# Batch 0 of a fused sigmoid attention and ReGLU kernel: values four passes behind scores, value casts on GpSimd, keys in two pieces, zero matmuls in gaps, and the last columns in two banks

## The chip, the cores and the metric

The kernel runs on one core of one Trainium2 chip. The metric is the device time of one execution in microseconds (us), as the median over repeated executions. Besides it there is the **span** that a profile shows, from the first to the last instruction of the execution that was profiled.

## The reference, cut to what matters

```python
def _attn_ref(q, k, v):                       # q, k, v: (8, 12, 448, 64) float32
    scores = np.matmul(q, k.transpose(0, 1, 3, 2)) / np.sqrt(64) - np.log(448)
    attn = 1.0 / (1.0 + np.exp(-scores))      # sigmoid, no softmax
    return np.matmul(attn, v)

def _moe_ref(x, w_gate, w_val, w_out):        # x: (3584, 768), d_ff = 1536
    gate = np.maximum(x @ w_gate, 0.0)
    return (gate * (x @ w_val)) @ w_out       # (3584, 768) float32
```

The output of the attention, heads side by side, is the input x of the second part, called the FFN below. Its product with `w_out` is the **down projection**.

## The kernel before: the parts concerned

Twelve heads of a batch are three blocks of four heads, so there are 24 blocks. A block is worked off in seven **passes**, one for each group of 64 keys: scores on TensorE (PE), the sigmoid on ScalarE (ACT), values on TensorE. Batch 0 (blocks 0 to 2, 21 passes) is a stage of its own. From then on the FFN of batch b runs on TensorE, and the passes of batch b + 1 are slipped in as **visits** between its matmuls.

```python
filler(40)                                   # 40 matmuls of 128 columns on the identity
cast_qk(0, "q", nc.vector, nc.scalar)
cast_qk(0, "k", nc.vector, nc.scalar)
for _ in range(4):
    start_next()                             # next weight load, and its cast on GpSimd
transposes(0, "q", nc.vector)
transposes(0, "k", nc.scalar, nc.vector)
cast_v(0, nc.vector)

LAG = 2
for i in range(NBLK * NCH + LAG):            # batch 0
    n, c = divmod(i, NCH)
    if n < NBLK:
        scores(n, c)
    if i >= LAG:
        m, cm = divmod(i - LAG, NCH)
        values(m, [cm])
    ...                                      # casts and transposes of block n + 1
    if i % 2 == 1 and i < NBLK * NCH:
        start_next()

def visit():
    i0 = state["pass"]
    n, c = divmod(i0, NCH)
    i1 = min(i0 + (3 if c == 0 else 2), NPASS)
    for i in range(i0, i1):
        if c == 0 and i == i0 + 2 and n > NBLK:
            values(n - 1, range(NCH))
        scores(*divmod(i, NCH))
    ...
```

`feed`, called by each visit, loads and casts later blocks. Blocks 3 to 5 are transposed on TensorE, blocks from 6 on by DMA. Loads are issued in program order, those of the first three blocks on two queues, all later ones on one. The last columns of the output are copied out of one bank of PSUM (the memory that TensorE writes its results to), half by ACT, half by VectorE (DVE).

## Time and profile before

| | the kernel before |
|---|---|
| median of the timed executions | 434.59 us (434.58 to 435.0) |
| the profiled execution: time | 437.15 us |
| the profiled execution: span | 434.6 us |
| TensorE busy | 421.6 us (97%) |
| first sigmoid starts, last sigmoid starts | 8.23, 26.66 us |
| first FFN matmul | 28.25 us |

The page itself has a sign of what was particular about that execution, the granted TensorE clock in tenths, over 40 slices of the span:

```profile
PEclk9989999999999999999999999999999999999999
```

The 8 in the third slice (21.7 to 32.6 us) means that the clock was not full there for part of the time.

The timeline of the last microseconds of the same profile shows the tail: start, length, engine, instruction, and in brackets the idle time before it with what ended it.

```profile
430.89 0.28 ACT L268 ACTIVATE ysb<-y_ps 128x128 f32<-128x128 f32 x1 [0.66 <-PE y_ps L251]
431.20 0.29 DVE L269 TENSOR_SCALAR ysb<-y_ps 128x128 f32<-128x128 f32 x1 [15.22 <-ACT ysb L268]
```

DVE waited for ACT, not for TensorE: both read the same PSUM bank, one after the other.

### The profile page before, as it was taken

The page shows a single profiled execution, that of the slowest core. Times are in us where ns is not written, and L with a number is a line of the kernel's source. Part 1 is how long each engine was busy: PE and PEld are TensorE (multiplying, and loading weights), DVE is VectorE, ACT ScalarE, POOL GpSimd, SP SyncE. Part 2 cuts the span into 40 slices and gives each one's busy share as a digit, 9 for nine tenths or more (in the row PEclk, how much of TensorE's full clock was granted, in tenths as well). Part 3 has the DMA queues.
Part 4 walks back from the last instruction along what each step waited for, and adds up shares of the span by engine and source line. Part 5 has one row for each costly group of instructions (what it writes and reads, how often), then busy time and mean ns, then how long its engine had stood idle before and what let it go on. Part 6 is the DMA issues. An engine that isn't in the chain of part 4 may idle for free.

```text
span 434.6 us, 7877 instructions
## 1 busy us (share of the span) xinstructions
PE 421.6 (97%) x3292; PEld 216.9 (50%) x3292; DVE 102.8 (24%) x172; ACT 235.6 (54%) x325; POOL 100.6 (23%) x130
## 2 busy tenths in 40 slices
PE   7779999999999999999999999999999999999996
PEld 5334554544455445544455454554455444455553
DVE  3632331123201322113211232023220232212210
ACT  5955656655566555555546556565555556532221
POOL 0287758213301313113031133023130100000000
PEclk9989999999999999999999999999999999999999
DMA  8999999791228910596216932199114320030014
GB/s 306 385 384 386 391 391 271 221 265 72 42 74 231 301 37 16 144 262 170 42 38 193 255 128 44 42 242 293 21 24 109 80 44 2 14 96 1 2 36 110
DMA packets 64100, 66.98 MB, mean 154 GB/s; under 512 B 35776, under 2 KB 54336, under 8 KB 64064
## 3 DMA queue, kind: packets, MB, share of 16 engines
q1 hardware_dynamic: 63088, 64.89, 51.2%
q10 hardware_dynamic: 976, 1.57, 1.0%
q8 instruction: 26, 0.43, 0.4%
q14 instruction: 10, 0.08, 0.1%
HBM read 47.19 MB, written 11.01 MB: 134 GB/s over the span
## 4 chain that ended last, share of the span: by engine, by line
PE 95%; ACT 4%; issue 1%; POOL 0%; DVE 0%; ACTq 0%; POOLq 0%
PE gv_ps L225 51%; PE y_ps L251 26%; PE qk_ps L172 9%; PE pv_ps L196 7%; ACT PT L182 3%; PE tr L157 1%; PE fill L336 1%; ACT gate_sb L237 0%; ACT kT L162 0%; POOL ident masks.py:199 0%; DVE ysb L269 0%; ACT ysb L268 0%; POOL ident masks.py:197 0%; POOL bias_t L63 0%; ACTq L182 0%
## 5 line engine op out<-in xcount | busy, mean ns | idle before, releaser
L182 ACT ACTIVATE PT<-qk_ps,bias_t 128x896 f16<-128x896 f32 x168 | 158.1, 1006 | 55.9 <-PE qk_ps L172 55.7
L225 PE MATMUL gv_ps<-xT,wg 128*128 128x448 f16 x576 | 128.5, 355 | 0.0
L225 PE MATMUL gv_ps<-xT,wv 128*128 128x448 f16 x576 | 128.3, 354 | 0.0
L251 PE MATMUL y_ps<-wo,hT 128*128 128x512 f16 (+1 forms) x672 | 114.1, 326 | 0.0
L237 ACT ACTIVATE gate_sb<-gv_ps 128x448 f32<-128x448 f32 x96 | 52.3, 544 | 93.5 <-PE gv_ps L225 93.5
L240 DVE TENSOR_TENSOR hT<-gate_sb,gv_ps 128x448 f16<-128x448 f32 x96 | 59.6, 621 | 168.7 <-PE gv_ps L225 135.8
L251 PEld LDWEIGHTS <-hT 128*128 128x128 f16 x672 | 64.0, 98 | 48.1 <-issue 7.5
L225 PEld LDWEIGHTS <-wv 128*128 128x128 f16 x576 | 54.8, 98 | 57.1 <-issue 9.1
L225 PEld LDWEIGHTS <-wg 128*128 128x128 f16 x576 | 55.0, 98 | 54.6 <-issue 7.1
L209 DVE TENSOR_SCALAR xT<-pv_ps 128x448 f16<-128x448 f32 x48 | 27.7, 620 | 133.1 <-PE pv_ps L196 133.0
L172 PE MATMUL qk_ps<-qT,kT 64*64 64x448 f16 x672 | 51.6, 360 | 6.6 <-ACT PT L182 6.0
L116 POOL CAST v<-st_v 128x448 f16<-128x448 f32 x21 | 11.8, 562 | 173.2 <-PE pv_ps L196 172.6
L273 ACT ACTIVATE ysb<-y_ps 128x512 f32<-128x512 f32 (+1 forms) x55 | 27.1, 493 | 40.6 <-PE y_ps L251 40.3
L196 PE MATMUL pv_ps<-PT,v 64*64 64x448 f16 x672 | 40.2, 351 | 1.3 <-ACT PT L182 0.8
L172 PEld LDWEIGHTS <-kT 64*64 64x64 f16 x672 | 15.8, 105 | 37.3 <-issue 33.0
L109 POOL CAST h16q<-st_q 128x896 f16<-128x896 f32 x21 | 19.6, 932 | 33.3 <-DMA kT<-h16k 32.5
L196 PEld LDWEIGHTS <-v 64*64 64x64 f16 x672 | 20.1, 107 | 13.5 <-issue 1.8
L109 POOL CAST h16k<-st_k 128x896 f16<-128x896 f32 x21 | 19.6, 932 | 1.3 <-DMA qT<-h16q 0.8
L141 POOL CAST wg<-st_wg 128x1536 f16<-128x1536 f32 x6 | 8.9, 1484 | 18.1 <-DMA st_wg<-in_moe_w_gate_dram 18.1
L117 POOL CAST v<-st_v 64x448 f16<-64x448 f32 x21 | 11.7, 559 | 1.3
L118 POOL CAST v<-st_v 64x448 f16<-64x448 f32 x21 | 11.7, 557 | 0.9
L141 POOL CAST wo<-st_wo 128x1536 f16<-128x1536 f32 x6 | 8.8, 1468 | 6.2 <-DMA st_wo<-in_moe_w_out_dram 6.2
(28 smaller groups left out, 51.6 us busy)
## 6 DMA issues: line engine op xcount, KB each, us to landing
st_q<-in_q_dram SPq DMA_DIRECT2D x24, 448.0 KB, 4.7
out_dram<-ysb SPq DMA_DIRECT2D x54, 192.0 KB, 2.7
st_v<-in_v_dram SPq DMA_DIRECT2D x23, 448.0 KB, 5.9
st_k<-in_k_dram SPq DMA_DIRECT2D x22, 448.0 KB, 5.2
st_wg<-in_moe_w_gate_dram SPq DMA_DIRECT2D x6, 768.0 KB, 11.9
st_wu<-in_moe_w_val_dram SPq DMA_DIRECT2D x6, 768.0 KB, 12.2
st_wo<-in_moe_w_out_dram SPq DMA_DIRECT2D x6, 768.0 KB, 11.9
st_k<-in_k_dram ACTq DMA_DIRECT2D x2, 448.0 KB, 6.6
```

Of the source, the lines that this page charges most:

```text
L109: eng.tensor_copy(o, i)
L116: eng.tensor_copy(t[:, 0], st[:, 0])
L141: eng.tensor_copy(dst, st[:])
L172: nc.tensor.matmul(ps[o : o + 64, bank, 0:S], kT[r : r + 64, c, h, :], qT[r : r + 64, :, h, :], start=True, stop=True, tile_position=(r, o ...
L182: nc.scalar.activation(pt[:], ps[:, :, 0:S], AF.Sigmoid, bias=bias_t[:], scale=qk_scale)
L196: nc.tensor.matmul(pv[pr][o : o + 64, 0:S], t[r : r + 64, pr, c * D : (c + 1) * D], pt[r : r + 64, pr, :], start=(c == 0), stop=(c == NCH ...
L209: nc.vector.tensor_scalar(out=x[:], in0=pv[pr][:, 0:S], scalar1=XSCALE, scalar2=None, op0=AOP.mult)
L225: nc.tensor.matmul(acc[:, 0:S], w[:, dc, jj * P : (jj + 1) * P], xT[b, dc][:], start=(dc == 0), stop=(dc == NDC - 1),)
L237: nc.scalar.activation(g_sb[:], acc[:, 0:S], AF.Relu)
L240: nc.vector.tensor_tensor(out=hT[f][:, o : o + S], in0=g_sb[:], in1=ps[1][:, 0:S], op=AOP.mult)
L251: nc.tensor.matmul(y[:, 0:mn], hT[f][:, o : o + P], wo[f // FG][:, f % FG, m0 : m0 + mn], start=(f == 0), stop=(f == NFC - 1),)
L273: nc.scalar.activation(ysb[:, m0 : m0 + mn], y[:, 0:mn], AF.Copy, scale=OUT_SCALE)
```

## The change

Its intent is to make the start of the FFN earlier and the end shorter. In batch 0 the values run four passes behind the scores (two at the end), the casts of the values move from DVE to GpSimd (POOL), block 0's keys are loaded and cast in two pieces, and zero matmuls fill gaps on TensorE to keep its clock up. The first FFN visit has two passes instead of three, block 6 is transposed on TensorE instead of by DMA, and the last 256 columns go to two banks. Cut to its core:

```diff
     def feed(i: int):
...
-        if c == 4 and NPRO <= m < NB:
+        if c == 4 and NPRO < m < NB:
             dma_transposes(m)
-        if c == 5 and NBLK < m < NPRO:
+        if c == 5 and NBLK < m <= NPRO:
             transposes(m, "k")
             transposes(m, "q")
...
-        i1 = min(i0 + (3 if c == 0 else 2), NPASS)
+        i1 = min(i0 + (3 if c == 0 and n > NBLK else 2), i0 + NCH - c, NPASS)
...
-        filler(40)
-        cast_qk(0, "q", nc.vector, nc.scalar)
-        cast_qk(0, "k", nc.vector, nc.scalar)
+        new_fill()
+        filler(*[512] * 10)
+        cast_qk(0, "q", nc.vector, nc.scalar, cut=(0, 4, NCH))
+        cast_qk(0, "k", nc.vector, nc.scalar, cut=(0, 2, 4))
+        transposes(0, "q")
+        filler(128, 128)
+        transposes(0, "k", nc.scalar, nc.vector, cut=(0, 2, 4))
...
+        cast_qk(0, "k2", nc.vector, cut=(4, NCH))
+        for n in range(NBLK):
+            cast_v(n, nc.gpsimd)
...
-        LAG = 2
-        for i in range(NBLK * NCH + LAG):
+        NP0 = NBLK * NCH
+        done = 0
+        for i in range(NP0 + 2):
             n, c = divmod(i, NCH)
             if n < NBLK:
                 scores(n, c)
-            if i >= LAG:
-                m, cm = divmod(i - LAG, NCH)
-                values(m, [cm])
+            while done <= i - (4 if i < NP0 - 4 else 2):
+                values(done // NCH, [done % NCH])
+                done += 1
...
+            if 1 <= i <= 3:
+                filler(256)
...
-            if c == 4 and n + 1 < NBLK:
-                transposes(n + 1, "k")
-                transposes(n + 1, "q")
-                cast_v(n + 1, nc.vector)
-            if i % 2 == 1 and i < NBLK * NCH:
+            if c in (3, 5) and n + 1 < NBLK:
+                transposes(n + 1, "k" if c == 3 else "q")
+            if 13 <= i < NP0:
                 start_next()
...
-                count = 3 * NBLK + (1 if b == 0 else 0)
+                count = 3 * NBLK + (2 if b == 0 else 0)
```

Cut out: the loads of k in two pieces, the two banks in `down`, and the order k before q in later loads.

More of the change, by code (lines that the diff above doesn't have):

```diff
@@ L86, in load_block, with cast_qk @@
         b, i = divmod(n, NBLK)
-        for nm, src, eng in which:
+        for nm, src, c0, c1, eng in which:
             st = stp.tile([P, 2, S], FP32, tag="st", name=f"st_{nm}")
-            eng.dma_start(
-                st[:],
-                src[b, i * HB : (i + 1) * HB].rearrange("(r h) (p c) d -> (h p) r (c d)", h=2, c=NCH),
-            )
+            rows = src[b, i * HB : (i + 1) * HB].rearrange("(r h) (p c) d -> (h p) r (c d)", h=2, c=NCH)
+            eng.dma_start(st[:, :, c0 * D : c1 * D], rows[:, :, c0 * D : c1 * D])
             staged[nm, n] = st
     def load_all(n: int):
-        load_block(n, ("q", q, nc.sync), ("k", k, nc.sync), ("v", v, nc.sync))
-    def cast_qk(n: int, nm: str, *engines):
+        load_block(n, ("k", k, 0, NCH, nc.sync), ("q", q, 0, NCH, nc.sync), ("v", v, 0, NCH, nc.sync))
+    def cast_qk(n: int, nm: str, *engines, cut=(0, NCH)):
         st = staged.pop((nm, n))
         h16 = h16p.tile([P, NCH, 2, D], FP16, tag="h16", name=f"h16{nm}")
-        cut = [0, 4, NCH] if len(engines) == 2 else [0, NCH]
         for c0, c1, eng in zip(cut, cut[1:], engines):
@@ L151, in dma_transposes, with transposes @@
             qkT[nm, n] = t2
-    def transposes(n: int, nm: str, *engines):
+    def transposes(n: int, nm: str, *engines, cut=(0, NCH)):
         h16 = qk16.pop((nm, n))
         tr = wkp.tile([P, NCH, 2, KC], FP16, tag="wk", name="tr")
-        for c in range(NCH):
+        for c in range(cut[0], cut[-1]):
             nc.tensor.transpose(tr[:, c], h16[:, c, :, :], ident[:])
-        t2 = qkTp.tile([P, NCH, 2, KC], FP16, tag="qkT", name=f"{nm}T")
-        cut = [0, 2, NCH] if len(engines) == 2 else [0, NCH]
+        t2 = qkT.get((nm, n)) or qkTp.tile([P, NCH, 2, KC], FP16, tag="qkT", name=f"{nm}T")
         for c0, c1, eng in zip(cut, cut[1:], engines or (nc.vector,)):
@@ L247, in down @@
         ysb = ysbp.tile([P, DM], FP32, tag="ysb", name="ysb")
+        last = col0 + P == B * S
         for m0, mn in ((0, 512), (512, DM - 512)):
-            y = wkp.tile([P, 512], FP32, tag="wk", name="y_ps")
+            nb = 2 if last and m0 else 1
+            w = mn // nb
+            ys = [wkp.tile([P, 512], FP32, tag="wk", name="y_ps") for _ in range(nb)]
             for f in range(NFC):
-                nc.tensor.matmul(
-                    y[:, 0:mn],
-                    hT[f][:, o : o + P],
-                    wo[f // FG][:, f % FG, m0 : m0 + mn],
-                    start=(f == 0),
-                    stop=(f == NFC - 1),
-                )
+                for j, y in enumerate(ys):
+                    c0 = m0 + j * w
+                    nc.tensor.matmul(
+                        y[:, 0:w],
+                        hT[f][:, o : o + P],
+                        wo[f // FG][:, f % FG, c0 : c0 + w],
+                        start=(f == 0),
+                        stop=(f == NFC - 1),
+                    )
                 if f < NFC - 1:
                     yield mn / 2400.0 + 0.002
-            rows = []
-            for half in range(2):
-                b, r = divmod(col0 + 64 * half, S)
-                o_rows = out[b * S : (b + 1) * S].rearrange("(p c) m -> c p m", c=NCH)
-                rows.append(o_rows[r // KC])
-            last = col0 + P == B * S
-            if last and m0 + mn == DM:
-                h = m0 + mn // 2
-                nc.scalar.activation(ysb[:, m0:h], y[:, 0 : mn // 2], AF.Copy, scale=OUT_SCALE)
-                nc.vector.tensor_scalar(
-                    out=ysb[:, h:DM], in0=y[:, mn // 2 : mn], scalar1=OUT_SCALE, scalar2=None, op0=AOP.mult
-                )
-            else:
-                nc.scalar.activation(ysb[:, m0 : m0 + mn], y[:, 0:mn], AF.Copy, scale=OUT_SCALE)
+            for j, y in enumerate(ys):
+                dst = ysb[:, m0 + j * w : m0 + (j + 1) * w]
+                if j == 0:
+                    nc.scalar.activation(dst, y[:, 0:w], AF.Copy, scale=OUT_SCALE)
+                else:
+                    nc.vector.tensor_scalar(out=dst, in0=y[:, 0:w], scalar1=OUT_SCALE, scalar2=None, op0=AOP.mult)
             if last or m0 + mn == DM:
@@ L276, in down @@
                 for half, eng in enumerate((nc.sync, nc.scalar if last else nc.sync)):
-                    eng.dma_start(rows[half][:, s0 : m0 + mn], ysb[64 * half : 64 * half + 64, s0 : m0 + mn])
+                    b, r = divmod(col0 + 64 * half, S)
+                    rows = out[b * S : (b + 1) * S].rearrange("(p c) m -> c p m", c=NCH)
+                    eng.dma_start(rows[r // KC][:, s0 : m0 + mn], ysb[64 * half : 64 * half + 64, s0 : m0 + mn])
             yield mn / 2400.0 + 0.002
@@ L331, in visit, with filler, new_fill @@
         state["pass"] = i1
-    def filler(count: int):
-        t = wkp.tile([P, 512], FP32, tag="wk", name="fill")
-        for _ in range(count):
-            nc.tensor.matmul(t[:, 0:P], ident[:], ident[:], start=True, stop=True)
+    zeros = const.tile([P, 512], FP16, name="zeros")
+    nc.vector.memset(zeros[:], 0.0)
+    fill: list = []
+    def filler(*widths):
+        for w in widths:
+            nc.tensor.matmul(fill[-1][:, 0:w], zeros[:, 0:P], zeros[:, 0:w], start=True, stop=True)
+    def new_fill():
+        fill.append(wkp.tile([P, 512], FP32, tag="wk", name="fill"))
     with tc.manual_schedule():
         nc.scalar.activation(warm[:], bias_t[:], AF.Sigmoid)
-        load_block(0, ("q", q, nc.sync), ("k", k, nc.scalar), ("v", v, nc.scalar))
-        load_block(1, ("q", q, nc.sync), ("k", k, nc.sync), ("v", v, nc.sync))
-        load_block(2, ("k", k, nc.scalar), ("q", q, nc.sync), ("v", v, nc.sync))
+        sp, act = nc.sync, nc.scalar
+        load_block(0, ("q", q, 0, NCH, sp), ("k", k, 0, 4, act), ("k2", k, 4, NCH, sp), ("v", v, 0, NCH, act))
+        load_block(1, ("k", k, 0, NCH, sp), ("q", q, 0, NCH, act), ("v", v, 0, NCH, sp))
+        load_block(2, ("k", k, 0, NCH, act), ("q", q, 0, NCH, sp), ("v", v, 0, NCH, sp))
         def halves(kind, j):
@@ L357, in start_next @@
                 cast_w(*what, nc.gpsimd)
-        filler(40)
-        cast_qk(0, "q", nc.vector, nc.scalar)
-        cast_qk(0, "k", nc.vector, nc.scalar)
+        new_fill()
[5 more added lines that the diff above has]
+        transposes(0, "k", nc.scalar, nc.vector, cut=(0, 2, 4))
+        new_fill()
+        filler(128, 128, 128)
+        cast_qk(0, "k2", nc.vector, cut=(4, NCH))
+        for n in range(NBLK):
+            cast_v(n, nc.gpsimd)
         for _ in range(4):
             start_next()
-        transposes(0, "q", nc.vector)
-        transposes(0, "k", nc.scalar, nc.vector)
-        cast_v(0, nc.vector)
-        LAG = 2
-        for i in range(NBLK * NCH + LAG):
+        NP0 = NBLK * NCH
+        done = 0
+        for i in range(NP0 + 2):
             n, c = divmod(i, NCH)
@@ L373 @@
                 scores(n, c)
-            if i >= LAG:
-                m, cm = divmod(i - LAG, NCH)
-                values(m, [cm])
+            while done <= i - (4 if i < NP0 - 4 else 2):
+                values(done // NCH, [done % NCH])
+                done += 1
+            if i == 2:
+                qk16["k", 0] = qk16.pop(("k2", 0))
+                transposes(0, "k", nc.vector, cut=(4, NCH))
+            if 1 <= i <= 3:
+                filler(256)
             if c == 1 and n + 1 < NBLK:
```

## The prediction

> **What bounds the kernel now.** I read the page first, then busy time in short windows, then the list of waits of TensorE, then the timelines of the first 75 us and the last 15, engine by engine. The page:
>
> ```profile
> PE 421.6 (97%) x3292; PEld 216.9 (50%) x3292; DVE 102.8 (24%) x172; ACT 235.6 (54%) x325; POOL 100.6 (23%) x130
> ...
> PE   7779999999999999999999999999999999999996
> ```
>
> TensorE (PE) is idle for 13 of 434.6 us only. The row of tenths puts these in the first three slices and the last. So a change can win only at the two ends, or where PE is busy but slow. From the list of PE waits over the first 45 us (us in total, times, longest):
>
> ```profile
> PE qk_ps L172 <- ACT PT L182: 6.0, 13, 1.0
> PE fill L336 <- POOL ident masks.py:199: 1.4, 1, 1.4
> ```
>
> The same list from 38 us to the end holds one wait of 1.0 us, the one that ends at 37.98, and nothing else. In the first 28 us (batch 0: 21 passes of scores, sigmoid, values) the sigmoids on ACT set the pace: the passes follow each other every 0.90 us (PE score starts 13.97, 14.87, 15.77, 16.67, 17.57), and PE works some 0.45 us in each. Sigmoid starts run from 8.23 to 26.66: 18.4 us for 20 steps, against 18.0 with no gap. Then the first FFN matmul, at 28.25. The windows around it:
>
> ```profile
> 28.00:29.00 1.00, 1.00 (x7) 0.31 (x4) 0.65 (x2) 0.00 (x0) 0.91 (x2) 0.50 1.05 381
> 29.00:30.00 1.00, 1.00 (x4) 0.43 (x3) 0.50 (x1) 0.00 (x0) 0.76 (x1) 0.50 1.04 383
> 30.00:31.00 1.00, 1.00 (x4) 0.46 (x3) 0.00 (x0) 0.29 (x1) 0.70 (x1) 0.50 1.04 381
> ...
> 34.00:36.00 2.00, 2.00 (x13) 1.03 (x11) 0.62 (x1) 0.54 (x1) 1.43 (x2) 1.00 1.05 380
> ```
>
> The columns are span, PE, weight loads, DVE, ACT, POOL, granted clock, DMA share, GB/s. The FFN starts at clock 0.50: 13 matmuls from 28.25 to 32.14 take 3.89 us, where 13 x 0.189 = 2.46 at the full rate (six took 1.13 later), so 1.43 us are lost. The DMA share is above 1 here, and it is so in every window from 3 to 70 us. That is the second limit, and the timeline of GpSimd (POOL) shows where it will bite:
>
> ```profile
> 62.03 1.47 POOL L141 CAST wo<-st_wo 128x1536 f16<-128x1536 f32 x1 [4.00 <-DMA st_wo<-in_moe_w_out_dram]
> 64.01 1.47 POOL L141 CAST wo<-st_wo 128x1536 f16<-128x1536 f32 x1 [0.52 <-DMA st_wo<-in_moe_w_out_dram]
> 65.96 1.47 POOL L141 CAST wo<-st_wo 128x1536 f16<-128x1536 f32 x1 [0.48 <-DMA st_wo<-in_moe_w_out_dram]
> ...
> 67.92 3.19 PE L251 MATMUL y_ps<-wo,hT 128*128 128x512 f16 x16
> ```
>
> The last piece of w_out is cast the moment it lands, at 65.96, and is ready at 67.43. The first output matmul that reads it is the eleventh of the down projection that starts at 67.92: 67.92 + 10 x 0.216 = 70.08. So the whole FFN of batch 0 can be pulled forward by only 70.08 - 67.43 = 2.65 us before PE waits for weights that no change of order has brought nearer.
>
> **What the skill says.** (1) "TensorE: Matmul & The Clock Gate", Part 1: the array runs at half rate until some 3.4 us of activity release it, and falls back after a window of little activity. The trace agrees: 0.60 on average over 28.40 to 31.85, 1.00 in the 3.41 us after. (2) "DMA: Bandwidth & Descriptors", "Issuing engines are not separate DMA queues": loads from several engines share the same 16 DMA engines. The trace agrees: 383 GB/s with two queues at work at 5 to 6 us, 387 with practically one from 10 to 70 us. (3) "SBUF — State Buffer", "SBUF: two separate sides": VectorE (in its fast modes) and GpSimd lock each other out for a whole instruction. The trace agrees: a value cast on DVE takes 0.39 us alone, 1.47 and 1.59 at 19.75 and 21.64, beside 1.47 us casts on POOL. (4) "PSUM — Partial Sum Buffer", "PSUM bank collisions raise a hardware error": two engines must not touch one bank at once, reads included. The trace shows the order kept: at the end DVE copies its half (0.29) only after ACT's half (0.28). That a collision would be an error, no run here shows.
>
> **The change, part by part.**
>
> First scores. Before: 40 matmuls on the identity run from 1.39 to 5.84 (0.111 each, cold) and hold up the q transposes, whose cast was done at 4.97; then k's seven transposes; scores at 7.80. After: ten 512-wide matmuls on zeros need only a DVE memset, so I let them run from 1.1 (an estimate) for 10 x 512/128 x 0.107 = 4.27 us, to 5.4. Seven q transposes at the cold 0.107: 6.1; two fillers: 6.35; only four k transposes: 6.8; ACT's 0.37 us copy: 7.15; scores at 7.2. Gain 0.6 us, first sigmoid near 7.6 (down to 6.8 if the clock opens early).
>
> The 21 passes. Value casts leave DVE (nine of 0.39, two stretched to 1.5, one of which held up values at 23.29). On POOL they cost 3 x 0.56 = 1.7 us a block; POOL is idle until 17.45, all three blocks fit before the first weights land, and values run four passes behind, so the first cast (v lands near 7 to 8.5) is needed only near 10.5. Transposes split over two passes keep ACT fed. I take 18.1 for the 20 steps (18.0 ideal). Last sigmoid ends 7.6 + 18.1 + 1.0 = 26.7 instead of 27.68. Values then take 0.2, and the last two DVE copies (1.16) hold the sixth matmul by some 0.35: effective FFN start 27.3.
>
> Clock. Before, the last two steps of the stage hold values alone (pass spacing 0.9, some 0.2 us of PE in each). After, twelve value matmuls come together with pass 17 and twelve at the end, so the last 3.4 us have more PE work (about 1.9 us against 1.4, by my count of the passes). I expect no drop: the effective start before was 28.25 + 1.43 = 29.68, after 27.3. That is 2.4 us. If the drop stays, 28.4.
>
> First FFN visit. Two passes instead of three: the 1.0 us wait for a score buffer at 37.98 goes.
>
> Unhindered, these sum to 2.4 + 1.0 = 3.4 us. Up to the eleventh down matmul both kernels do the same PE work: the order of instructions shows eight visits with 17 passes and two blocks of values in the new kernel, seven visits with the same 17 and two in the old; the eighth comes after the third down matmul. So it would be reached at 70.08 - 3.4 = 66.7. **But w_out is not there**: all the weights and blocks 0 to 6 are loaded ahead of the last piece in both, through DMA that is full from 3 us on. It comes no earlier; a little later, as k's first block is cut in pieces (a 1024 B packet takes 46 to 49 ns, a 1792 B one 74; an estimated 10 ns more a row, 16 rows an engine: 0.16). Ready at 67.6. PE waits some 0.9 us, and the gain is 70.08 - 67.6 = **2.5 us**.
>
> Block 6. Its two DMA transposes become 14 on PE, in the tenth visit, after that wait: 46.51 to 47.30 for the same set, **-0.8 us**, on the path since PE has no idle time there.
>
> End. Two banks let ACT and DVE copy at once: 0.29 + the gap saved, 0.31. 24 matmuls of 128 columns at 0.057 (warm transposes: seven in 0.40) are 1.37, 12 of 256 at 0.109 are 1.31. **+0.25**.
>
> Sum: 2.5 - 0.8 + 0.25 = 1.9; 434.6 - 1.9 = 432.7.
>
> **The rivals.**
>
> A. Weights don't bind (the last w_out lands earlier, or my count of PE work is off): the full 3.4 - 0.8 + 0.25 = 2.9, so 431.7. For it: SP's issue order is changed around w_out. Against: the same bytes lie ahead, and the landings in the trace follow the order of issue.
>
> B. The clock drops again at the FFN's start (0.5 x 3.4 us). Effective start 28.4, eleventh matmul at 67.8 instead of 67.6: it costs 0.2 us only, as the wait for w_out shrinks by the rest. 432.9.
>
> C. Lag 4 starves PE in passes 0 to 3 (no values there; the fillers are 256 wide) and the clock falls in mid-stage. At half rate a pass needs 0.9 us of PE, just what ACT allows; transposes would push it over. Start late by 1 to 2 us, 433.5 to 434.5. For it: values were four matmuls of the eight in a pass. Against: windows with half of PE's time used kept the full clock before.
>
> D. POOL's value casts stall DVE by the lock, or the v tile lands late and values stall PE. Against: both have 2 us or more to spare at 10 us.
>
> **Range and chances.** The cap by w_out makes the time insensitive to the early gains: any effective start before 28.1 gives 432.7. I give this 0.65, A 0.12, B and C together 0.2. Range 431.6 to 434.2. Two per cent is 8.7 us, more than all idle time that the change touches, and the order of instructions after block 6 shows no new work but the end's, so "same" is nearly certain.
>
> **What would show it.** First sigmoid near 7.6 and last ended near 26.7; clock 1.00 from 28 to 32; no ACT wait near 38; POOL idle until the same w_out landing near 66; one PE wait on POOL of about 0.9 us before 67.6; 14 more transposes near 73; at the end ACT and DVE copies at the same time. The prediction is wrong if the last w_out cast ends well off 67.6, if PE loses time in new waits after 68 us, or if the clock is at 0.5 anywhere past 10 us.

## The result, and the profile after

The new kernel takes **434.91 us** (median of 4, from 434.77 to 435.11) against 434.58 (4 executions) of the kernel before. The ratio is 1.0007, with a 95% interval from 0.999 to 1.0024: the same. Ratios and intervals in this document are worked out over the executions of the same rounds, so they are not quite the ratio of the medians that are quoted.

The result lies outside the predicted range of 431.6 to 434.2. Yet the span of the new kernel's profile is 432.7 us, the predicted number to the digit, and nearly all that was to be seen in it is there. The page has the clock at 9 throughout (it rounds down; 9 is full). It shows 9 before the first record of the clock too, here at 5.53 us, although the matmuls of that time run at half rate (in the first profile 0.111 us for 128 columns at the start, 0.057 later); and a mean clock does not count that time either.

```profile
span 432.7 us, 7894 instructions
...
PE 421.4 (97%) x3296; PEld 214.6 (50%) x3296; DVE 99.5 (23%) x168; ACT 235.4 (54%) x325; POOL 105.6 (24%) x139
...
PE   7789999999999999999999999999999999999996
...
PEclk9999999999999999999999999999999999999999
```

Windows of one microsecond, for TensorE alone (span, busy time, granted clock, DMA share, GB/s), show the start of the FFN at clock 1.00, where the profile of the kernel before had 0.50:

```profile
28.00:29.00 1.00, 0.82 (x5) 1.00 1.11 397
29.00:30.00 1.00, 1.00 (x9) 1.00 1.00 375
30.00:31.00 1.00, 1.00 (x17) 1.00 1.05 387
```

The list of TensorE's waits from 60 us to the end holds one line, the wait for the last cast of w_out, predicted as 0.9 and found as 0.4 us. The timeline of TensorE shows it ahead of the eleventh down matmul:

```profile
65.36 1.68 PE L252 MATMUL y_ps<-wo,hT 128*128 128x512 f16 x7
67.48 1.68 PE L252 MATMUL y_ps<-wo,hT 128*128 128x512 f16 x12 [0.44 <-POOL wo L137]
```

And at the end DVE now starts 0.11 us after ACT instead of 0.31, released by TensorE and not by ACT:

```profile
429.05 0.28 ACT L264 ACTIVATE ysb<-y_ps 128x128 f32<-128x128 f32 x1 [0.64 <-PE y_ps L252]
429.16 0.29 DVE L266 TENSOR_SCALAR ysb<-y_ps 128x128 f32<-128x128 f32 x1 [15.00 <-PE y_ps L252]
```

So from one profile to the other the span fell by 1.9 us, as reckoned, while the median time rose by 0.3. One of the two profiles must be of an execution that is not like the timed ones. None of the three signs by which the prediction wanted to be found wrong showed up: the last w_out cast ended at 67.43 us, there was no new wait after 68 us, and the clock was full from 5.53 us to the last matmul. No sign tested the baseline.

### The profile page after: what moved, and what is told of

Same layout as the page of the kernel before. It is cut to its first block, busy times and chain, and to the rows that moved or that the text cites. A ratio compares the mean times of both kernels' runs of the same rounds, so it can differ in the third digit from the quotient of the medians. Undisturbed runs are those within 1.5% of the kernel's fastest.

```text
span 432.7 us, 7894 instructions
## 1 busy us (share of the span) xinstructions
PE 421.4 (97%) x3296; PEld 214.6 (50%) x3296; DVE 99.5 (23%) x168; ACT 235.4 (54%) x325; POOL 105.6 (24%) x139
## 4 chain that ended last, share of the span: by engine, by line
PE 86%; DMA 6%; ACT 3%; POOL 2%; issue 1%; DVE 1%; SPq 0%; DVEq 0%; POOLq 0%
PE gv_ps L220 47%; PE y_ps L252 25%; PE qk_ps L167 8%; PE pv_ps L191 6%; DMA st_wo<-in_moe_w_out_dram 5%; ACT PT L177 3%; DMA st_k<-in_k_dram 2%; POOL wo L137 1%; PE tr L153 0%; POOL wg L137 0%; DVE xT L204 0%; SPq L90 0%; DVE h16q L105 0%; POOL v L112 0%; POOL v L114 0%
## 5 line engine op out<-in xcount | busy, mean ns | idle before, releaser
L252 PE MATMUL y_ps<-wo,hT 128*128 128x512 f16 (+2 forms) x684 | 114.5, 323 | 0.4 <-POOL wo L137 0.4
L112 POOL CAST v<-st_v 128x448 f16<-128x448 f32 x24 | 13.5, 562 | 180.4 <-PE pv_ps L191 171.1
L264 ACT ACTIVATE ysb<-y_ps 128x512 f32<-128x512 f32 (+2 forms) x56 | 27.4, 489 | 39.8 <-PE y_ps L252 39.5
L191 PE MATMUL pv_ps<-PT,v 64*64 64x448 f16 x672 | 39.0, 349 | 0.8 <-ACT PT L177 0.8
L114 POOL CAST v<-st_v 64x448 f16<-64x448 f32 x24 | 13.7, 570 | 1.0
L113 POOL CAST v<-st_v 64x448 f16<-64x448 f32 x24 | 13.4, 560 | 1.5
L137 POOL CAST wv<-st_wu 128x1536 f16<-128x1536 f32 x6 | 8.8, 1470 | 3.4 <-DMA st_wu<-in_moe_w_val_dram 3.4
```

The costliest lines, as they stand in the source:

```text
L114: eng.tensor_copy(t[64:128, 1], st[0:64, 1])
L137: eng.tensor_copy(dst, st[:])
L191: nc.tensor.matmul(pv[pr][o : o + 64, 0:S], t[r : r + 64, pr, c * D : (c + 1) * D], pt[r : r + 64, pr, :], start=(c == 0), stop=(c == NCH ...
L252: nc.tensor.matmul(y[:, 0:w], hT[f][:, o : o + P], wo[f // FG][:, f % FG, c0 : c0 + w], start=(f == 0), stop=(f == NFC - 1),)
L264: nc.scalar.activation(dst, y[:, 0:w], AF.Copy, scale=OUT_SCALE)
```

## The experiments

Twelve runs were made on chips, two of them of the unchanged kernels, each beside the kernel before in the same rounds. **Theory 1**: the profile of the kernel before shows an unusual execution, and the usual ones have neither the clock drop nor the late start that the change was credited with curing. **Theory 2**: the drop is in every execution, and the new kernel loses its gain elsewhere.

All profiled executions in one table. The first two columns of times come from the trace's record of the granted clock, the others from timelines. "Sixth FFN" is the start of the sixth FFN matmul, where the first waits of the stage are over; "eleventh down" that of the first matmul that reads the last piece of w_out (the start of its group plus 0.216 for each one before it). "At half" leaves out the time before the clock first opens and after the last matmul.

| run | clock full from | at half | first sigmoid | sixth FFN | eleventh down | span | time of this execution |
|---|---|---|---|---|---|---|---|
| before, first profile | 7.27 | 27.75-31.17 | 8.23 | 30.09 | 70.08 | 434.6 | 437.15 |
| e0, before again | 4.52 | none | 7.10 | 28.56 | 68.01 | 432.5 | 434.41 |
| after | 5.53 | none | 7.27 | 28.38 | 67.48 | 432.7 | 434.77 |
| h1, after again | 5.54 | none | 7.36 | 28.57 | 67.72 | 432.9 | 434.94 |
| e1 | 5.03 | none | 7.02 | 28.26 | 67.74 | 432.0 | 434.19 |
| e2 | 3.97 | none | 6.55 | 27.99 | 66.48 | 431.7 | 433.78 |
| e3 | 4.43 | 11.25-14.66, 28.32-31.73 | 6.72 | 29.92 | 69.31 | 433.6 | 435.81 |
| f1 | 7.03 | none | 8.15 | 29.23 | 67.73 | 432.3 | 434.39 |
| f2 | 4.08 | none | 7.17 | 28.55 | 67.99 | 433.4 | 435.70 |
| f3 | 6.16 | none | 7.57 | 28.30 | 66.79 | 431.1 | 433.26 |
| f4 | 4.55 | none | 7.28 | 28.50 | 66.99 | 431.5 | 433.43 |
| g1 | 4.03 | 10.86-14.27 | 7.33 | 30.86 | 69.35 | 433.7 | 435.81 |
| g2 | 13.44 | none | 7.96 | 30.90 | 70.35 | 434.9 | 436.76 |
| g3 | 6.43 | 9.84-16.67 | 7.86 | 32.70 | 72.15 | 436.7 | 438.48 |

### e0_before: the kernel before, unchanged

No edit.

> The kernel before, unchanged. Theory 1 (the profile was not typical): the profiled execution of the kernel before took 437.15 us, 2.6 above its timed ones, and only it fell into the half-rate stretch at 28.4 us. Then executions near 434.6 us have a mean clock of 0.998 or more and a span near 432.5, and if the profile falls on one of them its trace has clock 1.00 from 28 to 32 us, FFN matmuls at 0.189 us from the first, and reaches the eleventh down matmul near 68.5 us instead of 70.1. Theory 2 (the drop is in every execution, and the new kernel loses its gain elsewhere): clock 0.995 and the stretch at 0.50 in executions of 434.6 us too. Ratio 1.000 in both.

Six executions took from 434.41 to 436.89 us, median 435.11, and the 11 of the same kernel in its role as the comparison 434.26 to 436.27, median 434.59; ratio 1.0016 (0.9996 to 1.0035). The profile fell on the one of 434.41 us, a usual one. The windows at the start of the FFN:

```profile
28.00:29.00 1.00, 0.82 (x5) 1.00 1.05 387
29.00:30.00 1.00, 1.00 (x7) 1.00 1.05 387
30.00:31.00 1.00, 1.00 (x17) 1.00 1.04 383
```

and TensorE's timeline there:

```profile
27.25 1.12 PE L225 MATMUL gv_ps<-xT,wg 128*128 128x448 f16 x5
28.56 0.35 PE L225 MATMUL gv_ps<-xT,wg 128*128 128x448 f16 x1 [0.18 <-DVE xT L209]
...
35.90 0.38 PE L172 MATMUL qk_ps<-qT,kT 64*64 64x448 f16 x4 [0.98 <-ACT PT L182]
```

The clock is 1.00, the first five matmuls come at 27.25 us, and even the 0.18 us wait for the last copy is there, just as in the new kernel. This is Theory 1: an execution of the **old** kernel at 434.41 us has the start that the prediction reserved for the new one. What differs between executions of one kernel is when the clock opens (4.52 us here, 7.27 in the first profile), which moves the first sigmoid from 8.23 to 7.10, and whether it falls again. Theory 2 is out.

Of 50 executions of the kernel before in these rounds, 9 have a span of 434.4 to 434.7 us with a clock of 0.994 to 0.996, like the first profile; the other 41 lie between 432.4 and 433.8. So the first profile fell on about one execution in five. The mean clock alone doesn't tell the two kinds apart, as Theory 1 wanted: five executions between 434.25 and 434.50 us have 0.995 or 0.996 as well, that is, 3.0 to 4.8 us at half rate, more than the 1.6 us or less that any trace here has at half after its last matmul. So some stretches at half rate cost nothing that shows; where these were, no trace tells.

What lies outside of the span differs too. It is 1.82 to 1.97 us in most executions of the kernel before, 2.28 to 2.49 in five of the 50, 2.52 in the first profile, and 1.97 to 2.17 in the ten of the new kernel. So of the 0.36 us between e0's time and that of the new kernel's profiled execution, 0.17 are span and the rest is this difference, whose cause the traces don't show.

Measured against e0's profiled execution, the new kernel gains 0.18 us at the sixth FFN matmul (28.38 against 28.56) and 0.53 at the eleventh down matmul (67.48 against 68.01). Its span is 0.17 us longer. The rest must be lost between 68 us and the end.

### f2_pe6: one part alone, block 6 transposed on TensorE

```diff
 # the kernel before
-        if c == 4 and NPRO <= m < NB:
+        if c == 4 and NPRO < m < NB:
             dma_transposes(m)
-        if c == 5 and NBLK < m < NPRO:
+        if c == 5 and NBLK < m <= NPRO:
```

> The kernel before with one other part alone: block 6 transposed on TensorE. If TensorE is the bound from 38 us on, this costs the 14 transposes, 0.8 us: 435.4, span of a usual execution 433.3. Rival: they fall into slack and cost nothing, 434.6.

It took 435.65 us (435.46 to 437.57) against 434.54; ratio 1.0031 (1.001 to 1.0052). The interval lies above 1, so this part alone makes the kernel slower, by some 0.3%. In TensorE's timeline the transposes stand between two stretches of down matmuls with nothing idle beside them, and take 0.79 us (73.53 to 74.32):

```profile
73.53 0.56 PE L157 MATMUL tr<-ident,h16k 128*128 128x128 f16 x7
73.93 0.55 PE L157 MATMUL tr<-ident,h16q 128*128 128x128 f16 x7
74.32 1.91 PE L251 MATMUL y_ps<-wo,hT 128*128 128x256 f16 x14
```

Up to the eleventh down matmul it is like e0 (67.99 against 68.01), and its span is 0.9 us longer than e0's (433.4 against 432.5). The 0.8 us of the prediction hold for TensorE. Another 0.13 us come after its last matmul, in every trace with block 6 on TensorE (from there to the end of the span 3.89 us here, 3.76 in e0), for a reason that the traces don't show.

### e1_dmatr6: the new kernel without that part

```diff
 # the new kernel
-        if c == 4 and NPRO < m < NB:
+        if c == 4 and NPRO <= m < NB:
             dma_transposes(m)
-        if c == 5 and NBLK < m <= NPRO:
+        if c == 5 and NBLK < m < NPRO:
```

> The new kernel with block 6 transposed by DMA again, as before. Theory 1: the 14 transposes on TensorE near 73.5 us cost 0.8 us on the path, so 434.9 - 0.8 = 434.1, span near 431.9, no new wait after 68 us. Rival: the DMA transposes would come late among the loads and TensorE waits for them near 77 us; then no gain or a loss.

434.05 us (433.73 to 434.7) against 434.59; ratio 0.9985 (0.9969 to 1.0001). As expected (434.1), and no wait for the DMA transposes: the list of TensorE's waits from 68 us on has only the wait for w_out, of the group that is still running then. The same profile shows something else. The clock opened 0.5 us earlier than in the profile of the new kernel, and the sixth FFN matmul came 0.12 us earlier (28.26 against 28.38). But the eleventh down matmul came **later**:

```profile
65.24 1.68 PE L252 MATMUL y_ps<-wo,hT 128*128 128x512 f16 x7
67.74 1.47 PE L252 MATMUL y_ps<-wo,hT 128*128 128x512 f16 x10 [0.82 <-POOL wo L137]
```

The wait grew from 0.44 to 0.82 us: by 0.12 for the earlier start, and by 0.26 because the last cast of w_out began at 66.22 here and at 65.96 there. In this stage a faster start only makes TensorE wait longer for w_out. From the eleventh down matmul to the end of the span e1 takes 364.30 us, the new kernel 365.23: block 6 on TensorE costs 0.9 us here as well.

### e2_wout and e3_both: w_out ahead of block 6

```diff
 # e2: the new kernel; e3: the kernel e1
-                if order and step % 8 == 0:
+                if order and step % 3 == 0:
                     start_next()
```

Weights are started more often in the FFN's first steps. So all of w_out is issued before block 6, which is needed only later.

> The new kernel with all loads of w_out issued ahead of block 6 (weights started every 3 steps instead of every 8). Theory 1: the 0.44 us wait for the last w_out cast at 67.5 us goes, the last piece lands some 3.6 us earlier (near 62.5); 434.9 - 0.4 = 434.5. Rival (weights were the cap on everything gained): more than 1 us faster. Other rival: block 6 arrives too late for its casts and transposes, a new wait near 73 us.

> Both of these edits. Theory 1: they add up, 434.9 - 0.8 - 0.4 = 433.7, span near 431.5, TensorE with no wait from 28.5 us to the end, and 0.2% faster than the kernel before. Rival: block 6's DMA transposes, now behind w_out, come late: a wait near 77 us takes the gain.

e2 took 433.92 us (433.78 to 435.62) against 434.59, ratio 0.9987 (0.997 to 1.0004). Its last w_out cast began at 62.20 us instead of 65.96, and the wait is gone:

```profile
62.22 0.81 PE L252 MATMUL y_ps<-wo,hT 128*128 128x512 f16 x3
...
64.97 3.32 PE L252 MATMUL y_ps<-wo,hT 128*128 128x512 f16 x20
```

Seven of the twenty matmuls come before the eleventh, so that one starts at 64.97 + 7 x 0.216 = 66.48, a full 1.0 us earlier than in the new kernel: 0.39 from an earlier start, 0.44 from the wait, the rest small. The median is 1.0 us below the new kernel's too (433.92 against 434.91, from different rounds), where 0.4 were expected. That a start which is early by luck now counts would explain it, but is not shown: of e2's other executions there is no trace. Block 6 did not come too late.

e3, both edits, took **433.45 us** (433.38 to 435.81) against 434.59, ratio 0.9978 (0.9959 to 0.9998). It was expected at 433.7. Five of its six executions lie between 433.38 and 433.73. It has the lowest median here, 0.2% below the kernel before in the same rounds, and 1.4 below the new one, which ran in other rounds. Its profile fell on the sixth execution, of 435.81 us, with the clock at half twice:

```profile
11.00:12.00 1.00, 0.85 (x12) 0.63 1.07 391
12.00:13.00 1.00, 1.00 (x15) 0.50 1.06 380
13.00:14.00 1.00, 1.00 (x15) 0.50 1.06 387
...
29.00:30.00 1.00, 1.00 (x5) 0.50 1.10 395
30.00:31.00 1.00, 1.00 (x4) 0.50 1.00 373
```

So the new batch 0, with its four passes of lag and its zero matmuls, falls into the same drop as the old one at times. The change did not take the drop away. The first of the two stretches is the prediction's rival C: TensorE is busy all the time there, the 20 steps of the sigmoids take 19.98 us instead of 18.31 in the new kernel, and the FFN starts at 28.18 instead of 27.07.

### f1_visit and f4_visit_wout: the first visit alone, without and with w_out ahead

```diff
 # the kernel before; f4 has the edit of e2 besides
-        i1 = min(i0 + (3 if c == 0 else 2), NPASS)
+        i1 = min(i0 + (3 if c == 0 and n > NBLK else 2), i0 + NCH - c, NPASS)
...
-                count = 3 * NBLK + (1 if b == 0 else 0)
+                count = 3 * NBLK + (2 if b == 0 else 0)
```

> The kernel before with one part of the change alone: two passes in the first FFN visit (and one visit more). In its usual executions the kernel before reaches the eleventh down matmul at 68.0 us and w_out is ready at 67.3. If w_out caps the gain, the 1.0 us wait of TensorE near 36 us goes, but a wait for the last w_out cast of some 0.3 us comes, and 0.7 us are gained: 433.9. If it doesn't cap, 1.0 us: 433.6 and no wait on GpSimd.

> The kernel before with two passes in the first visit and w_out ahead of block 6: no cap left. Expected: the full 1.0 us of the wait, 433.6, no wait of TensorE on GpSimd. If so, the rest of the change (values four behind, value casts on GpSimd, zero matmuls, two pieces of k) and the end are worth no more than 433.6 - 433.45 = 0.2 us in usual executions. Rival: the rest is worth more, this one near 434.2.

f1 took 434.22 us (433.87 to 435.41) against 434.54, ratio 0.999 (0.9973 to 1.0007): not told apart from the kernel before. Its trace tells more. From the sixth FFN matmul to the eleventh down matmul it needs 67.73 - 29.23 = 38.50 us, where e0 needs 68.01 - 28.56 = 39.45. The part is worth 0.95 us on that stretch, the predicted 1.0. But whether the cap would have taken some of it, f1 can't say: in its profiled execution the clock opened at 7.03 us, the FFN started 0.67 us later than in e0, and w_out was there in time (its last cast began at 65.81 and took 1.47). On the cap f1 is inconclusive; e1 and e2 show it.

f4 took 434.35 us (433.43 to 435.79), ratio 0.9992 (0.9971 to 1.0013). The median fell between the two expectations and decides nothing, as four of its executions lie above 434.3 and two below 433.5. In its profiled execution, of 433.43 us, the stretch is 66.99 - 28.50 = 38.49 us, with no wait on GpSimd.

### f3_best: block 1's key transposes one pass later

In the new kernel the sigmoids of batch 0 are not without a gap. This is how the early first sigmoid is given back, in the new kernel's timeline:

```profile
9.40 0.63 DVE L105 CAST h16k<-st_k 128x896 f16<-128x896 f32 x1 [1.79 <-DMA st_k<-in_k_dram]
9.94 0.62 DVE L105 CAST h16q<-st_q 128x896 f16<-128x896 f32 x1
10.08 0.56 PE L153 MATMUL tr<-ident,h16k 128*128 128x128 f16 x7 [0.26 <-DVE h16k L105]
10.48 0.88 DVE L159 COPY kT<-tr 128x384 f16<-128x384 f16 x2
10.88 0.38 PE L167 MATMUL qk_ps<-qT,kT 64*64 64x448 f16 x4 [0.23 <-DVE kT L159]
...
11.32 1.91 ACT L177 ACTIVATE PT<-qk_ps,bias_t 128x896 f16<-128x896 f32 x2 [0.35 <-PE qk_ps L167]
```

Block 1's keys land at 9.4 us. Their transposes stand in TensorE's queue ahead of the scores of pass 4, wait for the cast, and the scores and the sigmoid behind them wait too: this was the theory. The lines have a rival to it. The scores of pass 4 are the first that need the second piece of block 0's keys, and its copy (the first of the two at 10.48, 0.35 us long) stands on DVE behind both casts of block 1, the first of which waits for its data. The edit, on the kernel e3, moves the transposes and leaves the order on DVE:

```diff
-            if c in (3, 5) and n + 1 < NBLK:
-                transposes(n + 1, "k" if c == 3 else "q")
+            if c in (4, 5) and n + 1 < NBLK:
+                transposes(n + 1, "k" if c == 4 else "q")
```

> The new kernel with block 6 on DMA, w_out ahead of block 6 (433.45 us so far), and block 1's k transposes one pass later (pass 4 instead of 3). In the new kernel these stand ahead of the scores of pass 4 in TensorE's queue and wait for k to land near 9.4 us, so the earlier first sigmoid is given back in a 0.35 to 0.7 us gap on ACT. If that is so, the gap goes, the first FFN matmul comes 0.3 us earlier, and the time is 433.1. Rival: ACT is held elsewhere (values for want of v), no gain: 433.45.

In the profiled execution the gap is gone. All 21 sigmoids run without a break of the engine:

```profile
7.57 19.06 ACT L177 ACTIVATE PT<-qk_ps,bias_t 128x896 f16<-128x896 f32 x21 [0.49 <-PE qk_ps L167]
```

The first sigmoid came 0.30 us later than in the new kernel (7.57 against 7.27, for the clock opened later), and the sixth FFN matmul still came 0.08 us earlier (28.30 against 28.38). Two of six executions took 433.24 and 433.26 us, the shortest times. But the other four took from 434.73 to 435.89. The median is 434.83 and the ratio 1.0002 (0.9979 to 1.0025). The kernel is not better for the edit on the whole. Nor is its theory shown. Block 1's keys landed at 8.96 us in this execution and the first sigmoid came later, so the copy was done before ACT ran out of scores. In g1 below, which has this edit, the keys land at 9.39, and a gap of 0.66 us on ACT is back. And in all seven traces of the new batch 0 (the new kernel twice, e1, e2, e3, f3, g1) the scores of pass 4 start 0.05 to 0.06 us after that copy on DVE ends (10.88 after 10.83 in the new kernel, 11.05 after 10.99 in g1), so the traces speak for the rival. An edit that moves the copy ahead of the casts was not run.

The slow executions have no trace, but their mean clock is 0.996, 0.992, 0.996 and 0.996, against 1.000 of the two fast ones. That is about 3.4 us at half rate, and twice that in one. At which stage is not shown.

### g2_nowarm: the kernel before without its warm-up

```diff
-        filler(40)
```

> The kernel before without its 40 warm-up matmuls. If the time at which the clock opens sets the first sigmoid and what follows, it opens later (7 us or after), the first sigmoid starts at 8.2 us or later instead of 7.1, and the time is 1 us or more above 434.5, with a drop near 28 us more often. Rival: the loads alone set the start; transposes come 0.3 us earlier without the warm-up in their way, and the time is the same or better.

436.76 us (435.99 to 436.97) against 434.60; ratio 1.004 (1.0025 to 1.0056). The trace has the clock at full only from 13.44 us on, and the sixth FFN matmul at 30.90 us, 2.3 us later than in e0. What was wrong is the mechanism at the start: the first sigmoid came at 7.96 us, not at 8.2 or later, since the transposes no longer queue behind the warm-up. It is the passes up to 13.4 us at half rate that cost the time: ACT runs out of scores at 12.80 and goes on only at 13.94. And no drop came near 28 us. This run shows directly what the moment at which the clock opens is worth: 8.9 us of delay cost about 2.2.

### g1_best_zeros and g3_before_zeros: more zero matmuls in batch 0

```diff
 # in values(); g1: the kernel f3, g3: the kernel before
+        if n < NBLK and chunks[-1] < NCH - 1:
+            for _ in range(4):
+                nc.tensor.matmul(pv[0][:, S:512], zeros[:, 0:P], zeros[:, 0 : 512 - S],
+                                 start=False, stop=False, skip_group_check=True)
```

> The best kernel so far (profiled execution 433.26 us, timed ones from 433.24 to 435.89) with four more zero matmuls of 64 columns in each pass of batch 0, written to unused columns of the values' bank. If the slow executions are clock drops for want of TensorE activity, some 0.2 us more activity in each 0.9 us pass keeps the clock up: all executions within about 1 us of 433.2, none at 435 or more, and no 0.50 after 8 us in the trace. Rival (the slow executions have another cause): the same spread, 433.2 to 435.9.

> The kernel before with the same zero matmuls in its passes. If drops make its slow executions (435 to 437 us), they go and all lie between 434.2 and 435.3, the rest of the spread being the time at which the clock opens. Rival: the same spread up to 437.

Both missed. g1 took 434.95 us (434.1 to 435.81; ratio 1.0, 0.9981 to 1.002), half of its executions above 435.6. g3 took 436.01 (435.66 to 438.48; ratio 1.0029, 1.0009 to 1.0049), slower than without. Neither trace has a drop near 28 us, but both have an early one, g1 from 10.86 to 14.27 us and g3 from 9.84 to 16.67. In g1 it follows an idle stretch of TensorE (windows: span, busy, clock, DMA share, GB/s):

```profile
9.00:10.00 1.00, 0.75 (x7) 1.00 1.04 376
10.00:11.00 1.00, 0.00 (x0) 0.93 1.07 382
11.00:12.00 1.00, 0.95 (x10) 0.50 1.07 385
```

There TensorE waited for the second piece of block 0's keys, whose copy stood on DVE behind the casts of block 1 (see f3), and zeros that come with the values, from pass 4 on, can't help. Once the clock is at half, the added matmuls take time that the passes need. Whether zeros prevent the late drop can't be told from one trace of each; that they prevent slow executions is refuted in this form.

### h1_after: the new kernel again

No edit.

> The new kernel again, for its spread. From the parts: against a usual execution of the kernel before it gains about 0.5 us up to the eleventh down matmul (the cap of w_out), loses 0.8 us on block 6's transposes and gains 0.1 to 0.2 at the end, so usual executions near 434.8, with slower ones up to 437 where the clock drops, as in the kernel before. Rival (the change removes the drops): no execution above 435.3, while the kernel before has some in the same rounds.

434.86 us (434.57 to 436.08) against 435.04 (434.39 to 436.51); ratio 1.000 (0.9979 to 1.002). The expected 434.8 holds. Two executions of six, 435.43 and 436.08, were slow, with a mean clock of 0.996 and 0.992: the new kernel has drops too. In this round the kernel before had 4 of 11 at 435.2 or more. So nothing here shows that the new kernel is slow less often; e3 and f3, with the same batch 0 or nearly so, had slow ones too.

## Why the prediction was wrong, point by point

**The step that failed is the last line of the sum, "434.6 - 1.9 = 432.7", through the term that it rests on, the start of the FFN.** The gain was worked out between the profiled execution of the kernel before and the new kernel, and was then taken from the median of timed executions. The profiled execution took 437.15 us. From there, 437.15 - 1.9 = 435.25 is within 0.5 of the 434.77 that the new kernel's profiled execution took, and the rest lies outside of the span (2.52 us there, 2.07 here). The span of 434.6 that I read on the page happened to equal the median of 434.59 and hid the mistake.

That the span of the new kernel's profile is 432.7 is in part luck. Between the two profiles the terms hold: the eleventh down matmul came 2.60 us earlier (2.5 predicted), block 6 cost 0.9 (0.8), the end gave 0.23 (0.25). But the early start behind the first of them was there without the change, in e0.

Term by term, against a usual execution of the kernel before (e0):

| step of the prediction | predicted | measured | by |
|---|---|---|---|
| effective start of the FFN | 2.4 us | 0.18 us | sixth FFN matmul, 28.56 to 28.38 |
| first visit, no third pass | 1.0 | 0.95 | f1 against e0 on the same stretch |
| slack until w_out binds | 2.65 | 0.7 | e0: eleventh down matmul 68.01, last cast done 65.82 + 1.47 = 67.29 |
| gain at the eleventh down matmul | 2.5 | 0.53 | 68.01 to 67.48, after a wait of 0.44 |
| block 6 on TensorE | -0.8 | -0.9 | eleventh down matmul to the end of the span: 365.45 (f2) against 364.53 (e0), 365.23 (new) against 364.30 (e1); 0.79 of it are the transposes |
| end, two banks | 0.25 | 0.23 | the same stretch, 364.30 (e1) against 364.53 (e0; 364.55 in f1, so the visit has no part in it); the copies end 1.86 us after the last 512-wide copy starts in e0, 1.64 in the new kernel |
| sum | 1.9 | about -0.2 | 0.53 - 0.92 + 0.23; the spans are 432.54 and 432.71 |

**First scores and first sigmoid.** The gain of 0.6 us, from 8.23 to 7.6, was for a cold clock until 7.3. In e0 the clock opened at 4.52 and the old kernel's first sigmoid was at 7.10, earlier than the new one's 7.27. The prediction did note that the new start would be earlier "if the clock opens early", but applied it to one side only. Where the clock opens at nearly the same time, the new start is 0.4 to 0.6 us earlier: 6.72 (e3, 4.43) against 7.10 (e0, 4.52) and 7.28 (f4, 4.55), and 6.55 (e2, 3.97) against 7.17 (f2, 4.08). So the 0.6 us were about right for like executions.

**The 21 passes.** "18.1 for the 20 steps" was 18.3 in the new kernel, with the gap before pass 4 (see f3); it was 18.7 in e0. That part was about right, and worth 0.4 us; with a first sigmoid that is 0.17 later, 0.18 of it are left at the sixth FFN matmul.

**Clock.** "I expect no drop" came true in the new kernel's two profiles, though not in every execution (h1). It is true of the old kernel's usual executions as well (e0, f1, f2 and f4, all with the old batch 0, have no drop, and 41 of 50 spans show no such loss), so the 1.43 us were not the change's to gain. The reason given for it fails too: in the last 3.41 us before the FFN, TensorE is busy for 1.92 us in the new kernel and for 1.92 in e0, where the prediction counted 1.9 and 1.4. Rival B asked what would follow if the drop stayed in the new kernel. The rival that was missing is that it is mostly not in the old one. Rival C is seen in e3, D in no trace: TensorE never waits for v in the new kernel's profile.

**The cap by w_out** was right as a mechanism and is shown by e1 and e2: the wait of TensorE on GpSimd, the longer wait after an earlier start, and the faster kernel when w_out is loaded sooner. Its size was off with the baseline: usual executions were already within 0.7 us of it. "A little later" fits: the last cast began at 65.96, 66.20 and 66.22 us in the traces of the new batch 0 with the old order of loads (the new kernel twice, e1), and between 65.70 and 65.96 in those of the old batch 0.

**Block 6 and the end** held in kind and nearly in size. The loss of 0.9 us, which looked like a small deduction from 2.5, is what cancels the 0.53 us and the end.

**What decides over a drop** can be narrowed down from the traces. Between two changes of the clock lie 3.41, 6.83, 13.65 or 20.48 us, multiples of 3.41, counted from the moment at which it opens. Cut into such pieces, batch 0 and the FFN's start show this: each of the five falls from the full clock came at the end of a piece with little work, in which TensorE was busy for 1.89 us (the first profile, 24.34 to 27.75), 1.97 and 1.99 (e3), 1.60 (g1) and 1.77 (g3). Five other pieces had 1.93 to 2.02 us and kept the clock, and all the rest had 2.1 or more. So near 1.9 to 2.0 us either happens, and where the pieces fall depends on when the clock opened: e0's, from 25.00 to 28.41, already held FFN matmuls, and had 2.40.

What stays open: why the clock opens anywhere between 4.0 and 7.3 us from one execution to the next (13.44 without the warm-up), and what tells the pieces near 1.9 to 2.0 us apart. In g1 and g3 the passes with zeros have 2.8 us or more, but the thin piece lay before them.

## What to carry to other kernels

Before a gain is read off a profile, set the profiled execution beside the timed ones: if it is slower by as much as the gain at stake, whatever is particular in it (here a half-rate stretch and a late clock) belongs to that execution and not to the kernel. Where a transfer stream is full from the start, find the first consumer of its last piece and subtract the slack there from every gain upstream; reordering the stream (w_out ahead of a block that is needed later) was worth more here than the earlier start. Work put on the busiest engine to spare a DMA costs its full length: here 0.9 us, more than the rest of the change won.

## What the Trainium skill lacked or had wrong

- "TensorE: Matmul & The Clock Gate", Part 1, says that the clock falls back after an idle window of about 3.4 us. Here it fell at 27.75 us after 3.41 us in which TensorE was not idle: the windows of the first profile have it busy for 1.89 us from 24.34 to 27.75 (matmuls on a quarter of the array). The other falls in these traces followed 1.60 to 1.99 us of work in 3.41, and five times 1.93 to 2.02 us kept the full clock. What the page lacks is that a window that is half busy can end in a fall, and near which share.
- The same part calls the ramp variable from run to run and less than 1% of a typical span. Both hold here: the full clock came at 4.52 us in one profile of the kernel before and at 7.27 in another, and its executions lie between 434.3 and 437.2 us, 0.7%. What is lacking is that this can be more than the gain of a late tuning step, so that two profiles are not to be compared before their clocks are.
- No page gives the difference between the timed duration of an execution and its span from first to last instruction. "Runtime: NRT & Kernel Launch" has a gap, the same for every kernel, between two other quantities. Here the difference varied: 1.9 us (432.5 and 434.4) and 2.6 us (434.6 and 437.15) for the kernel before, and 1.97 to 2.17 for the new one.
